# Wider query groups, wider spatial passes, one gelu batch and new durations for the static scheduler of a two-layer attention and gMLP kernel

## Chip, cores, metric

One NeuronCore of one Trainium2 chip (trn2). The metric is the device time of one execution in microseconds (us). Profiles come from one execution of each kernel.

## The reference, cut to what matters

Two layers, each a multi-query attention with 32 heads of 16 and one shared key and value head, then a gated MLP whose gate is a product over all 2048 tokens (the "spatial" product).

```python
def _A_ref(x, wq, wk, wv, wo):                    # S = 2048, D = 512, H = 32, Dh = 16
    q = (x @ wq).reshape(B, S, H, Dh).transpose(0, 2, 1, 3)
    k = x @ wk; v = x @ wv                        # one key/value head for all
    scores = einsum("bhqd,bkd->bhqk", q, k) * Dh ** -0.5
    o = einsum("bhqk,bkd->bhqd", softmax(scores), v)
    return o.transpose(0, 2, 1, 3).reshape(B, S, H * Dh) @ wo

def _B_ref(x, w_in, w_sp, b_sp, w_out):           # Fh = 896
    z = gelu(x @ w_in)
    z1, z2 = z[..., :Fh], layernorm(z[..., Fh:])
    g = einsum("ts,bsf->btf", w_sp, z2) + b_sp[None, :, None]
    return (z1 * g) @ w_out

for _ in range(2):
    x = x + _A_ref(layernorm(x), ...)
    x = x + _B_ref(layernorm(x), ...)
```

## The kernel before

Tokens are handled in chunks of 512, 512, 512, 256, 128 and 128. Per layer, 2048 blocks of scores (128 keys x 512 columns) need an exponential. ScalarE (ACT) takes most of them, three and two banks of PSUM at a time; VectorE (DVE) takes the rest with a chain of seven instructions. Behind this run, on the same engines, the projections, layer norms, gelus and spatial passes of the chunks already done. After the last attention chunk of a layer there is a **closing**, in which the last chunk's MLP, the rest of the spatial products and the output projection must end before the next layer can start.

All this is ordered by a **static list scheduler that runs at build time**. Every operation has a duration; the scheduler simulates the engines with those durations, always takes the ready operation of the best priority, and the resulting order per engine is the program. PE executes strictly in that order. So a charge in this model changes none of the instructions that do the work; it changes where they stand, and with that how many warming matmuls are put in and whether ACT or DVE takes a block. One stream inserts these warming matmuls (results thrown away) wherever the model thinks that PE's activity in the last 3.41 us (a constant of the kernel's code) falls short.

The charges (cut):

```python
def job(self, pieces, cons, ...):             # side work on PE: projections, spatial passes
    ...
    prev = self.op("pe", ..., dur, ...)       # counts dur * 2400 columns of activity

def d_mm(n):                                  # charge for one matmul of n columns
    return max(n, 64) / 2400.0

# fill = the score matmuls of one ACT instruction; n = columns of the chunk, ns = 512 // n
o = k.sc.op("pe", fn, 0.32 + 0.05 * (ns - 1), deps, ..., slow=0.53 + 0.05 * (ns - 1))
# PV of one unit (four heads x 512 columns)
o = k.sc.op("pe", fn, (0.23 if self.u % 2 == 0 else 0.32) + 0.05 * (ns - 1), ...)
```

What a block is in a small chunk, and the wide spatial pass (cut):

```python
def _qk(self, e, b, bank):        # one block: ns key tiles of n columns side by side
    for s, kt in enumerate(b.unit.kts):
        ins = e.matmul(self.b32(bank)[:, s * n:(s + 1) * n],
                       self.kT[32*j:32*j+32, kt*128:(kt+1)*128],
                       self.qs[32*j:32*j+32, g.q.slot, g.qoff:g.qoff + n], tile_position=(32*j, 0), ...)

# spatial: 8 token groups of 256; two feature tiles per PSUM bank; weights double-buffered, 512 KB a load
for tc in range(8):
    ld = self.dma(... self.wsT[:, 8*sl:8*sl+nst, :] <- self.ws_dv[:, s0:s1, tc*256:(tc+1)*256])
    for f0 in range(0, NF, 2):
        ... e.matmul(o_[256 columns], self.z2n[:, s, f*128:(f+1)*128], w) for s in range(s0, s1)

# mixer_chunk: every chunk's gelu on its own, between two table loads
def gl(e):
    e.activation(z1v, z1v, ACTF.Gelu_apprx_tanh)
    return e.activation(z2f[...], z2f[...], ACTF.Gelu_apprx_tanh)
```

The softmax here doesn't subtract the row's maximum and nothing guards it: scores larger than these inputs give would overflow.

Of the kernel before, what the change touches and what calls it, by code (L numbers as in the profile page):

```python
# [57 lines left out]
class Sched:  # L58
# [217 lines left out]
    def job(self, pieces, cons, deps, prio, sem="side", piece_deps=None):  # L276
# [3 lines left out]
        for i, (fn, dur) in enumerate(pieces):  # L280
            dd = list(deps) if i == 0 else [prev]
            if piece_deps is not None:
                dd += piece_deps[i]
            prev = self.op("pe", (lambda e, fn=fn: fn(e, j.bank.idx)), dur, dd, prio if i == 0 else min(prio, CONT), sem=sem, job=j,
                           first=(i == 0), soft=[d for c in cons for d in c.get("deps", ())] if i == 0 else ())
# [79 lines left out]
GPL = 0  # L365
MERGE = 9
# [20 lines left out]
def d_mm(n):  # L387
    return max(n, 64) / 2400.0


class Group:
    __slots__ = ("layer", "ci", "hg", "t0", "n", "units", "q", "qoff", "evac", "index")


class QSet:

    __slots__ = ("groups", "op", "slot", "left", "reads", "index")


class Unit:  # L400
    __slots__ = ("grp", "kts", "blocks", "pv", "index", "last", "first")
# [6 lines left out]
class Kern:  # L408
    def __init__(self, nc, A_x, A_wq, A_wk, A_wv, A_wo, B_x, B_w_in, B_w_sp, B_b_sp, B_w_out, out):
# [12 lines left out]
        self.merge = MERGE  # L422
# [11 lines left out]
        self.ident16 = sb([P, P], FP16, "ident16")  # L434
# [10 lines left out]
        self.b8 = sb([8, 256], BF16, "b8")  # L445
# [26 lines left out]
        self.gp = sb([P, 8, NF, 256], FP16, "gp")  # L472
# [10 lines left out]
        self.ws_n = 0  # L483
# [49 lines left out]
    def load(self, A_x, A_wq, A_wk, A_wv, A_wo, B_b_sp):  # L533
# [20 lines left out]
        self.l_b = self.dma(lambda e: e.dma_start(self.b8[:], B_b_sp.rearrange("(k t) -> k t", k=8)), (), "ldb", 4096)  # L554
# [11 lines left out]
        for tc in range(8):  # L566
            for f in range(NF):
                self.gp_read[(tc, f)] = [o for o in free]
# [7 lines left out]
        self.c_id16 = sc.op("pool", lambda e: e.tensor_copy(self.ident16[:], self.ident[:]), 0.3, [self.c_id], 0.9)  # L576
# [111 lines left out]
    def layer_groups(self, layer):  # L688
        t0 = 0
        for ci, n in enumerate(self.chunks):  # L690
            nsub = 512 // n
            for hg in range(8):
                g = Group()
                g.layer, g.ci, g.hg, g.t0, g.n = layer, ci, hg, t0, n
                g.index = len(self.groups)
                if hg % nsub == 0:
                    qs = QSet()
                    qs.groups, qs.op, qs.left, qs.reads = [], None, 0, []
                    qs.index = len(self.qsets)
                    qs.slot = qs.index % NQS  # L700
                    self.qsets.append(qs)
                g.q = self.qsets[-1]
                g.qoff = (hg % nsub) * n
                g.q.groups.append(g)
                g.units = []
                g.evac = None
                for k in range(self.NT // nsub):
                    u = Unit()
                    u.grp = g
                    u.kts = list(range(k * nsub, (k + 1) * nsub))  # L710
                    u.index = len(self.units)
                    u.first = (k == 0)
                    u.last = (k == self.NT // nsub - 1)
                    u.pv = None
# [7 lines left out]
                g.q.left += 4 * len(g.units)  # L722
# [8 lines left out]
    def q_released(self, q):  # L731
        nx = q.index + NQS
        if nx < len(self.qsets):
            q2 = self.qsets[nx]
            if q2.groups[0].layer == 0 or q2.groups[0].layer == q.groups[0].layer or self.l1_ready:
                self.make_q(q2, q.reads)
            else:
                self.q_wait.append((q2, q.reads))
# [4 lines left out]
    def make_q(self, q, war=()):  # L743
        sc = self.sc
        g = q.groups[0]
        n = g.n

        def pe(e, b, h):
            ins = None
            for g2 in q.groups:  # L750
                for kd in ((0, 1), (2, 3))[h] if n == 512 else range(4):
                    if n == 512 or (g2.hg - g.hg) // (len(q.groups) // 2) == h:
                        ins = e.matmul(self.b32(b)[:, g2.qoff:g2.qoff + n], self.wq_pad[:, kd, g2.hg, :],  # L753
# [7 lines left out]
        pe_last, (op,) = sc.job([((lambda e, b: pe(e, b, 0)), 2 * d_mm(512)), ((lambda e, b: pe(e, b, 1)), 2 * d_mm(512))],  # L761
# [8 lines left out]
    def finish_group(self, g, pv_last):  # L770
        sc = self.sc
        n = g.n
        nq = n // 128
        par = self.evac_n % 2
        self.evac_n += 1
        ev = sc.op("dve", lambda e: e.tensor_copy(self.oT[:, par, 0:n], self.b32(self.pvb)[:, 0:n]), d_psum(n),  # L776
# [3 lines left out]
        def pe(e, b):  # L780
            ins = None
            for qt in range(nq):
                ins = e.transpose(self.b16(b)[:, qt * 128:(qt + 1) * 128], self.oT[:, par, qt * 128:(qt + 1) * 128],
                                  self.ident[:])
            return ins

        def rc(e, b):
            return e.reciprocal(self.rden[:, par, 0:nq, :], self.b16(b)[:, 0:nq * 128].rearrange(
                "p (qt j r) -> p qt j r", qt=nq, j=4)[:, :, :, DH])

        def nm(e, b):
            return e.tensor_tensor(  # L792
                self.on[:, 0:nq, g.hg * 64:(g.hg + 1) * 64].rearrange("p qt (j d) -> p qt j d", d=DH),
                self.b16(b)[:, 0:nq * 128].rearrange("p (qt j r) -> p qt j r", qt=nq, j=4)[:, :, :, 0:DH],
                self.rden[:, par, 0:nq, :, None].to_broadcast([P, nq, 4, DH]), ALU.mult)
        pl, (r, m) = sc.job([(pe, nq * 0.06)], [
            dict(fn=rc, dur=0.09 + nq * 4 * 8.4e-3, prio=0.6, deps=[self.rd_read[par]]),
            dict(fn=nm, dur=d_psum(nq * 64), prio=0.5, deps=[d for qt in range(nq) for d in self.on_read[qt]])],
            [ev, self.c_id], 1.2)
        self.oT_read[par] = pl  # L800
        self.rd_read[par] = m
        g_norm = m
        self.norms.append(g_norm)
        if g.hg == 7:
# [56 lines left out]
    def mixer_chunk(self, g):  # L861
# [37 lines left out]
        c0 = g.t0 % 512 if g.ci == self.merge + 1 else 0  # L899
        z1v = (self.z1L if last else self.z1s[:].rearrange("p (f t) -> p f t", f=NF))[:, :, c0:c0 + n]  # L900
        z1_war = list(self.dx_s.end) if last else list(self.z1s_free)
# [26 lines left out]
        if g.ci == self.merge:  # L928
            self.held = (T, z1, z2)
            return  # L930
        t0 = T[0]
        if g.ci == self.merge + 1:
            T, z1, z2 = [a + b for a, b in zip(self.held, (T, z1, z2))]
            t0, T = T[0], T
            z1v = self.z1s[:].rearrange("p (f t) -> p f t", f=NF)[:, :, 0:128 * len(T)]
# [3 lines left out]
        def gl(e):  # L939
            e.activation(z1v, z1v, ACTF.Gelu_apprx_tanh)  # L940
# [4 lines left out]
        else:  # L945
            gs = z1 = [sc.op("act", gl, d_act(NF * nt * 128) + d_act(nt * FH), z1 + z2, -1.0, table="gelu")] * (2 * nt)
        sp = self.dma(lambda e: e.dma_start(self.z1_dv[:, :, t0 * 128:(t0 + nt) * 128], z1v), z1,
                      f"z1s{g.layer}{g.ci}", nt * P * P * NF * 2)
        if last:
            self.z1L_spill = sp  # L950
        else:
            self.z1s_free = [sp]
        self.z1_spill.append((t0 * 128, (t0 + nt) * 128, sp))
# [15 lines left out]
        for (s0, s1, ci) in self.passes:  # L969
            if ci == g.ci:  # L970
                self.spatial(s0, s1, g.layer, final=False)
        if last:
            self.spatial(self.s_fin, self.NT, g.layer, final=True)
# [8 lines left out]
    def spatial(self, s0, s1, layer, final):  # L982
        sc = self.sc
        acc = s0 > 0
        pr = 2.0 if final else (2.5 if s1 > 8 else 4.0)
        if final:
            self.kv_war_from_layer()
            self.l_wout = self.dma(lambda e: e.dma_start(self.w_out_r, self.w_out_d.rearrange("(c p) n -> p c n", p=P)),
                                   [o for o in self.dx_s.end], "ldw", 917504, pr)
            self.hT_read = [[o for o in self.dx_s.end], [o for o in self.dx_s.end]]  # L990
        z1r = self.z1s[:].rearrange("p (k f t) -> p k f t", k=2, f=NF)
        zl = [list(self.z1s_free), list(self.z1s_free)]
        nst = s1 - s0
        early = not final and nst < 4
        gp_pe = final and layer < GPL
        z2f = self.z2n[:].rearrange("p t f -> p (t f)")
        if early:

            slot0 = self.wsT[:, 0:8, :].rearrange("p s t -> p (s t)")
            self.wsP = []  # L1000
            nf = self.NT - s1
            parts = [(0, 4, z2f[:, 2048:5120], (2, 3, 4, 5)), (4, 6, z2f[:, 5120:6656], (5, 6, 7)),
                     (6, 8, slot0[:, 0:1536], None)]
            if nst == 2:
                parts = [(0, 4, z2f[:, 4096:6144], (4, 5, 6)), (4, 8, slot0, None)]
            for (c0, c1, w_, tiles) in parts:
                w_ = w_.rearrange("p (s t) -> p s t", s=nst)
                war = self.last_ws[0] if tiles is None else [o for t in tiles for o in self.z2_read[t]]
                ld = self.dma(lambda e, w_=w_, c0=c0, c1=c1: e.dma_start(w_, self.ws_dv[:, s0:s1, 256 * c0:256 * c1]),
                              war + self.ws_st[s0:s1], f"wsp{c0}", (c1 - c0) * nst * 65536, 1.0)  # L1010
                for tc in range(c0, c1):
                    self.wsP.append((w_[:, :, 256 * (tc - c0):256 * (tc - c0 + 1)], ld, tiles))
            self.held_f = range(0, 3 if nf == 1 else 5)
            self.wsF = z2f[:, 0:2048 * nf].rearrange("p (s t) -> p s t", s=nf)
            self.wsF_ld = self.dma(lambda e: e.dma_start(self.wsF, self.ws_dv[:, s1:self.NT, :]),
                                   [o for t in self.held_f for o in self.z2_read[t]] + self.ws_st[s1:], "wsf", nf * 524288, 1.5)
        for tc in range(8):
            if final:
                lds = [self.wsF_ld]
                ws = [(s, self.wsF[:, s - s0, tc * 256:(tc + 1) * 256]) for s in range(s0, s1)]  # L1020
                held = self.held_f
            elif early:
# [622 lines left out]
```

## Time and profile before

| | before |
|---|---|
| time | 1915.69 us median of 3 runs (1913.76 to 1916.67) |
| instructions | 41204, of them 17275 matmuls |
| busy share | PE 85%, DVE 93%, ACT 92% |
| mean granted PE clock, profiled run | 0.974 |

From the page of the kernel before: busy time by engine, then groups of instructions. Columns of a group: line, engine, operation, what it writes and reads, count, busy time, mean ns of one, idle time of the engine just before it and who ended most of it.

```profile
PE 1634.2 (85%) x17275; PEld 655.4 (34%) x17275; DVE 1774.8 (93%) x3265; ACT 1767.6 (92%) x1573; POOL 59.3 (3%) x106
...
L1305 ACT ACTIVATE Pa<-ps_all 128x1536 bf16<-128x1536 f32 (+1 forms) x1437 | 1643.0, 1348 | 56.9 <-PE ps_all L1591 46.4
L1591 PE MATMUL ps_all<-qs,kT 32*128 32x512 bf16 (+2 forms) x6144 | 577.7, 317 | 225.6 <-ACT Pa L1305 207.8
...
L1488 DVE TENSOR_SCALAR E<-ps_all 128x512 int32<-128x512 f32 x505 | 343.7, 684 | 28.2 <-PE ps_all L1591 25.9
```

ACT's exponentials (line 1305) and DVE's (505 blocks, begun by line 1488) fill both engines. ACT does 4096 - 505 = 3591 blocks in 1643 us: 0.457 us each.

Where the time is lost is seen by stage. The windows view of the kernel before; each row is a stretch, its length, the busy time of each engine in it, the granted PE clock and the DMA load. The stretches: chunk 0's end and chunk 1; the wide spatial pass; the small chunks; then, in layer 1, chunk 0 undisturbed, chunk 1 with gelus, the wide pass, the small chunks; last the closing.

```profile
core 0: us, PE busy (x) PEld busy (x) DVE busy (x) ACT busy (x) POOL busy (x), PEclk, DMA share, GB/s
300.00:555.00 255.00, 205.67 (x1543) 58.38 (x1544) 246.62 (x431) 243.76 (x206) 6.70 (x8) 0.95 0.04 12
555.00:785.00 230.00, 216.41 (x2343) 97.04 (x2343) 208.83 (x368) 219.12 (x186) 3.55 (x6) 0.97 0.08 23
785.00:906.00 121.00, 104.49 (x2393) 65.41 (x2392) 102.89 (x215) 116.88 (x103) 4.46 (x8) 0.97 0.17 52
1022.00:1247.00 225.00, 182.47 (x1456) 49.64 (x1456) 222.60 (x381) 224.20 (x200) 2.27 (x4) 1.00 0.00 1
1247.00:1503.00 256.00, 212.12 (x1598) 60.64 (x1596) 237.19 (x410) 247.55 (x211) 6.13 (x8) 0.95 0.04 13
1503.00:1667.00 164.00, 156.23 (x1621) 70.38 (x1619) 149.00 (x259) 156.69 (x136) 1.88 (x4) 1.00 0.08 23
1667.00:1853.00 186.00, 158.76 (x3110) 91.34 (x3109) 161.79 (x326) 178.72 (x154) 6.63 (x10) 0.95 0.13 41
1853.00:1915.00 62.00, 53.40 (x405) 33.98 (x402) 53.10 (x126) 19.39 (x39) 1.56 (x4) 1.00 0.28 83
```

The undisturbed stretch 1022 to 1247 has ACT busy 99.6% at full clock: nothing to gain there. In the six other attention stretches ACT is idle 11.2 + 10.9 + 4.1 + 8.5 + 7.3 + 7.3 = 49.3 us (length less busy time).

The waits of the kernel before (engine, line, whom it waited for: us in total, times, longest):

```profile
ACT Pa L1305 <- PE ps_all L1591: 46.4, 93, 2.4
ACT E L1107 <- PE ps_all L1066: 43.2, 10, 8.1
...
DVE st_19 L956 <- ACT z2n L941: 10.4, 8, 2.6
```

The first is exponentials waiting for score matmuls, the second is the closing.

What narrow matmuls cost is read from start to start in PE's timeline (start, us to the modelled end, what, count), here in a 128-column chunk of the kernel before:

```profile
851.34 0.42 PE L1591 MATMUL ps_all<-qs,kT 32*128 32x128 bf16 x12
851.70 0.41 PE L1384 MATMUL ps_all<-Pa,V 128*32 128x128 bf16 x16
852.04 0.61 PE L1066 MATMUL ps_all<-wsT,z2n 128*128 128x256 bf16 x4
```

Twelve score matmuls of 128 columns (three blocks) hold PE for 0.36 us; the median over all such fills is 0.353 us, against 0.323 us for three matmuls of 512. The scheduler charged this fill 0.47.

One gelu in ACT's timeline of the kernel before: two table loads around two gelus, 8.9 us without an exponential.

```profile
1261.27 1.28 ACT L940 ACT_TABLE_LOAD   x1
1262.56 3.19 ACT L940 ACTIVATE z1s<-z1s 128x3584 bf16<-128x3584 bf16 x1
1265.66 3.17 ACT L941 ACTIVATE z2n<-z2n 128x3584 bf16<-128x3584 bf16 x1
1268.85 1.28 ACT L1305 ACT_TABLE_LOAD   x1
```

### The profile page before, as it was taken

What the parts mean: (1) busy time and instruction counts of PE and PEld (TensorE: products, weight loads), DVE (VectorE), ACT (ScalarE), POOL (GpSimd) and SP (SyncE); (2) the same over time, 40 slices, a digit from 0 to 9 for tenths busy, and PEclk for the clock granted to TensorE, in tenths of its full rate; (3) what the DMA queues carried; (4) which work ended last, traced back from release to release, by engine and by line L of the source; (5) the groups of instructions that cost most, each with busy time, mean ns of one, the idle gap of its engine ahead of it and who ended that gap; (6) DMA issues with size and microseconds to landing.
All of it is one profiled execution on the core that took longest, in us unless ns stands there. A gap on an engine that the chain in (4) does not pass through costs nothing.

```text
span 1914.8 us, 41204 instructions
## 1 busy us (share of the span) xinstructions
PE 1634.2 (85%) x17275; PEld 655.4 (34%) x17275; DVE 1774.8 (93%) x3265; ACT 1767.6 (92%) x1573; POOL 59.3 (3%) x106
## 2 busy tenths in 40 slices
PE   6887887788889998988988788888788999988898
PEld 3222222122234443555642122222122444335564
DVE  7999999999998898987999999989999898989968
ACT  6999999999999999999389999999999999999973
POOL 3000000000000000000010000000000000000000
PEclk9999999999999999999999999989998999999899
DMA  9700001000010100022200000010000010000213
GB/s 265 192 1 1 1 1 42 1 1 1 1 31 23 34 7 26 14 64 59 64 1 1 1 1 1 1 42 1 1 1 20 23 34 18 8 26 14 64 54 107
DMA packets 98041, 59.83 MB, mean 31 GB/s; under 512 B 39736, under 2 KB 94272, under 8 KB 97856
## 3 DMA queue, kind: packets, MB, share of 16 engines
q1 hardware_dynamic: 96272, 56.64, 10.5%
q8 instruction: 137, 2.24, 0.5%
q10 hardware_dynamic: 1584, 0.56, 0.1%
q14 instruction: 48, 0.39, 0.1%
HBM read 30.97 MB, written 17.83 MB: 25 GB/s over the span
## 4 chain that ended last, share of the span: by engine, by line
ACT 34%; PE 28%; DVE 24%; issue 12%; POOL 1%; ACTq 0%; DVEq 0%; POOLq 0%
ACT Pa L1305 32%; PE ps_all L1591 8%; PE ps_all L1066 7%; PE ps_all L1384 5%; DVE E L1488 4%; DVE Pd L1526 3%; DVE E L1524 2%; DVE E L1521 2%; DVE E L1515 2%; PE ps_all L1574 2%; PE ps_all L1135 2%; ACT z2n L941 1%; PE ps_all L753 1%; DVE E L1518 1%; DVE gp L1090 1%
## 5 line engine op out<-in xcount | busy, mean ns | idle before, releaser
L1305 ACT ACTIVATE Pa<-ps_all 128x1536 bf16<-128x1536 f32 (+1 forms) x1437 | 1643.0, 1348 | 56.9 <-PE ps_all L1591 46.4
L1591 PE MATMUL ps_all<-qs,kT 32*128 32x512 bf16 (+2 forms) x6144 | 577.7, 317 | 225.6 <-ACT Pa L1305 207.8
L1591 PEld LDWEIGHTS ps_all<-qs,kT 32*128 32x128 bf16 x6144 | 173.7, 93 | 710.4 <-ACT Pa L1305 627.7
L1488 DVE TENSOR_SCALAR E<-ps_all 128x512 int32<-128x512 f32 x505 | 343.7, 684 | 28.2 <-PE ps_all L1591 25.9
L1384 PE MATMUL ps_all<-Pa,V 128*32 128x512 bf16 (+2 forms) x5421 | 332.7, 317 | 2.1 <-DVE oT L776 1.6
L1526 DVE SCALAR_TENSOR_TENSOR Pd<-E 128x1024 uint16<-128x1024 int32 (+1 forms) x253 | 306.8, 1213 | 0.8
L1574 PE MATMUL ps_all<-wo_r,zero 128*128 128x512 bf16 (+2 forms) x923 | 250.0, 371 | 2.2 <-DVE E L1488 1.8
L1066 PE MATMUL ps_all<-wsT,z2n 128*128 128x256 bf16 x1428 | 216.4, 278 | 6.0 <-DVE on L792 2.7
L1384 PE MATMUL ps_all<-Pd,V 128*32 128x512 bf16 (+2 forms) x723 | 182.5, 327 | 0.0
L1521 DVE TENSOR_TENSOR E<-E 128x1024 f16<-128x1024 f16 (+1 forms) x253 | 172.9, 683 | 3.3
L1524 DVE TENSOR_TENSOR E<-E 128x1024 f16<-128x1024 f16 (+1 forms) x253 | 172.6, 682 | 2.3
L1515 DVE TENSOR_SCALAR E<-E 128x1024 f16<-128x1024 uint16 (+1 forms) x253 | 172.7, 684 | 1.1
L1066 PEld LDWEIGHTS ps_all<-wsT,z2n 128*128 128x128 bf16 x1428 | 117.2, 98 | 74.3 <-issue 35.6
L1384 PEld LDWEIGHTS ps_all<-Pa,V 128*32 128x32 bf16 x5421 | 98.8, 96 | 119.4 <-issue 101.6
L1574 PEld LDWEIGHTS ps_all<-wo_r,zero 128*128 128x128 bf16 x923 | 70.2, 99 | 121.3 <-issue 91.3
L1518 DVE TENSOR_SCALAR E<-E 128x1024 f16<-128x1024 f16 (+1 forms) x253 | 105.6, 417 | 2.6
L1517 DVE TENSOR_SCALAR E<-E 128x1024 f16<-128x1024 f16 (+1 forms) x253 | 105.6, 417 | 2.2
L1090 DVE TENSOR_TENSOR gp<-ps_all,gp 128x512 f16<-128x512 f32 (+1 forms) x128 | 76.2, 615 | 18.1 <-PE ps_all L1066 17.7
L753 PE MATMUL ps_all<-xnTA,wq_pad 128*128 128x512 bf16 (+2 forms) x384 | 69.9, 311 | 2.2 <-DVE E L1488 2.0
L1107 ACT ACTIVATE E<-ps_all 128x512 f16<-128x512 f32 (+1 forms) x58 | 26.2, 563 | 43.2 <-PE ps_all L1066 43.2
L881 PE MATMUL ps_all<-w_in_r,xnTB 128*128 128x448 bf16 x256 | 63.2, 356 | 2.0 <-DVE E L1488 1.2
L910 PE MATMUL ps_all<-xnTB,w_in_r 128*128 128x512 bf16 (+2 forms) x336 | 62.9, 311 | 1.3 <-DVE z1s L921 1.0
(83 smaller groups left out, 1171.1 us busy)
## 6 DMA issues: line engine op xcount, KB each, us to landing
wsT_scratch<-gp SPq DMA_DIRECT2D x16, 512.0 KB, 3.7
wsT<-wsT_scratch SPq DMA_DIRECT2D x16, 512.0 KB, 4.0
z1s<-z_scratch SPq DMA_DIRECT2D x16, 448.0 KB, 3.9
z_scratch<-z1s SPq DMA_DIRECT2D x6, 896.0 KB, 4.0
wsT<-wsT_scratch SPq DMA_DIRECT2D x16, 256.0 KB, 2.9
X<-in_A_x_dram SPq DMA_DIRECT2D x8, 256.0 KB, 6.6
out_dram<-X SPq DMA_DIRECT2D x16, 128.0 KB, 1.7
w_in_r<-in_B_w_in_dram SPq DMA_DIRECT2D x1, 1792.0 KB, 10.9
```

What stands on the lines that cost most here:

```text
L1066: ins = e.matmul(o_, self.z2n[:, w[0], f * 128:(f + 1) * 128], w[1], start=st, stop=sp_)
L1305: return e.activation(k.Pa[:, base:base + n, :], k.b32(b0, n).rearrange("p (k q) -> p k q", k=n), ACTF.Exp, scale=SCALE)
L1384: ins = e.matmul(k.b32(k.pvb)[32 * j:32 * j + 32, 0:n], k.V[:, kt, 32 * j:32 * j + 32], b.slot[:, s * n:(s + 1) * n], tile_position=(0, 32 ...
L1488: return k.sc.op("dve", lambda e: e.tensor_scalar(k.eI[:, s, 512 * i:512 * (i + 1)], k.b32(j.bank.idx)[:, 0:512], C_LOG2, C_BIAS, op0=ALU. ...
L1515: return lambda e: e.tensor_scalar(out, a, m, None, op0=ALU.mult)
L1517: return lambda e: e.tensor_scalar(out, a, b, None, op0=ALU.add)
L1518: return lambda e: e.tensor_scalar(out, a, m, b, op0=ALU.mult, op1=ALU.add)
L1521: o4 = sc.op("dve", lambda e: e.tensor_tensor(q, u, w, ALU.mult), d_sb(n, 0.521e-3), [o3], pr)
L1524: o6 = sc.op("dve", lambda e: e.tensor_tensor(q, q, u, ALU.mult), d_sb(n, 0.521e-3), [o5], pr)
L1526: o7 = sc.op("dve", lambda e: e.scalar_tensor_tensor(po.bitcast(U16), I, 2.0 ** -9, q, op0=ALU.mult, op1=ALU.add), d_sb(n, 1.042e-3), [o6] ...
L1574: ins = e.matmul(k.b32(k.pvb if b is None else b.idx)[:, 0:n], k.zero[:], k.wo_r[:, 0, 0:n], start=b is not None, stop=b is not None)
L1591: ins = e.matmul(self.b32(bank)[:, s * n:(s + 1) * n], self.kT[32 * j:32 * j + 32, kt * 128:(kt + 1) * 128], self.qs[32 * j:32 * j + 32, g ...
```

## The change

Four parts:

- **Groups**: in a small chunk, 2 or 4 head groups lie side by side as 512 query columns against one key tile, so that every score and PV matmul is 512 wide. With it the extra charge for narrow fills and PV units goes.
- **Spatial**: the spatial passes take 512 tokens per matmul (4 token groups in place of 8, one feature tile per bank, the widest pass with a single-buffered 1 MB weight load).
- **Merge**: chunk 0's gelu waits for chunk 1's; both run between one pair of table loads.
- **Durations**: the scheduler's charges for side matmuls, and the columns that it counts for them.

```diff
             prev = self.op("pe", ...,
-                           first=(i == 0), ...)
+                           cols=dur * 1900.0, first=(i == 0), ...)      # Durations
 def d_mm(n):
-    return max(n, 64) / 2400.0
+    return max(n / 2400.0 + 0.006, min(0.045 + n * 0.43e-3, 0.155))
 ... layer_groups:                                                        # Groups
-            nsub = 512 // n
-            for hg in range(8):
+            nh = 512 // n
+            for hg in range(0, 8, nh):
-                for k in range(self.NT // nsub):
-                    u.kts = list(range(k * nsub, (k + 1) * nsub))
+                for k in range(self.NT):
+                    u.grp, u.kt, u.index, u.pv = g, k, len(self.units), None
 ... fill and PV:
-        o = k.sc.op("pe", fn, 0.32 + 0.05 * (ns - 1), deps, ...)
+        o = k.sc.op("pe", fn, 0.32, deps, ...)
-        o = k.sc.op("pe", fn, (0.23 if self.u % 2 == 0 else 0.32) + 0.05 * (ns - 1), ...)
+        o = k.sc.op("pe", fn, 0.23 if self.u % 2 == 0 else 0.32, ...)
 ... mixer_chunk:                                                         # Merge
-        if g.ci == self.merge:          # merge was 9: never
+        if g.ci == 0:
+            self.held = (T, z1, z2, z1v)                                 # z1 kept in gp's place
+            return
+        if g.ci == 1:
+            T, z1, z2 = [a + b for a, b in zip(self.held[:3], (T, z1, z2))]
 ... spatial:                                                             # Spatial
-        for tc in range(8):
-            for f0 in range(0, NF, 2):  # 256 columns
+        nsl = 1 if nst > 4 else 2
+        for tc in range(4):
+            for f in range(NF):         # 512 columns
(cut: storage of gp and bias, the closing split off as its own method, the group's finish)
```

## The prediction

> **What bounds the kernel.** The page gives ScalarE (ACT) 92% and VectorE (DVE) 93% busy over 1914.8 us, PE 85%. Both evaluate the softmax exponentials: by the groups, 1437 ACT ops (1643 us, 2.5 blocks of 512 columns each, 0.457 us a block) and 505 DVE blocks (seven ops, about 2.7 us a block). In the undisturbed stretch 1000-1260 (the windows) ACT is busy 99.6%, DVE 98%: 2.55 blocks/us. It falls to 2.3 in the two wide spatial passes (560-720, 1480-1640; PE 154 of 160 us) and 2.1-2.3 in the small chunks (720-900, 1640-1840; DVE idle about 40 us in all, ACT 14). Over both attention phases ACT idles about 58 us; 46 us of it "exp waits for the score matmuls" (the waits). The two closings (ACT idle about 75 us) are hardly touched.
>
> **What the change does.**
> 1. QK and PV fall from 6144 to 4096 matmuls each. Start-to-start times in the trace say that this saves little PE time: three score blocks take 0.323 us at 512 wide, 0.331 as six of 256, 0.352 as twelve of 128; two PV units 0.548, 0.554, 0.563. Over about 300 such fills: some 6 us of PE, with PV under 2, off the critical path. The Trainium skill ("TensorE: Matmul & The Clock Gate", Back-to-back issue gap) gives N/2.4 + 2.5 ns warm; the trace agrees (0.109 us per 256-wide spatial matmul): columns, not instructions, are paid.
> 2. Spatial passes: half the matmuls, twice as wide. Four of 256 with the switch take 0.543 us; two of 512 (the w_in groups) 0.538. No gain. The 8-tile weight load becomes single-buffered 1 MB (512 KB lands in 4 us): three gaps of perhaps 8 us per layer, which only spread the pass.
> 3. Finishing small head groups: 48 become 16 in both layers, about 7 us of DVE less, worth 1-2 us, since DVE does a seventh of the exponentials. Fewer waits of PV for the evacuation.
> 4. Gelu of chunks 0 and 1 together: one pair of 1.283 us table loads less per layer: 5.1 us of ACT, on the path, worth 4.5. Against it: one ACT stall of about 15 us in place of two of 9; DVE, whose blocks come only with fills, idles 2.4 us in one of 9 and will idle some 8.
> 5. The static schedule is built with other PE durations. It charged small-chunk fills 0.37/0.47 us against 0.33/0.35 in the trace; afterwards 0.32, about right. Better ordering may recover part of the ACT idle time in small chunks and spatial passes (32 us) and at gelus: I take 8 us. Side matmuls count as fewer columns, so a few more warming matmuls.
>
> **Sum.** 4.5 (tables) + 1.5 (DVE) + 8 (ordering, fewer group ends) + 2 (PE relief feeding DVE) - 1.5 (longer gelu stall) = 14.5 us, 0.8%.
>
> Predicted 1901 us, range 1882 to 1917. Faster by over 2%: 0.10; within 2%: 0.87; slower by over 2%: 0.03.
>
> **What would show it.** Table loads at the gelu line 10 -> 8; QK and PV 4096 each; PE busy down only a few per cent, still near 96% in the spatial stretches; DVE evacuations 96 -> 64; ACT exp still 0.457 us a block; steady stretch still 2.55 blocks/us; small-chunk stretches shorter by 5-10 us in both layers together; closings the same to 3 us.
>
> **What would make it wrong.** If narrow matmuls hold PE longer than starts show, the gain reaches 30-40 us. If the merged gelu lets the clock fall, or the single-buffered passes drag spatial work into the closing, it vanishes. The schedule is a greedy list: any change of durations reshuffles it, a few us either way.

## The result, and the profile after

| | before | after |
|---|---|---|
| time, median | 1916.18 us (4 runs, 1913.76 to 1919.03) | 1885.68 us (4 runs, 1884.69 to 1889.73) |
| ratio | 1 | 0.9844 (95%: 0.9824 to 0.9865) |
| matmuls | 17275 | 12178 |
| mean granted clock, fast runs | 0.9755 (40 runs) | 0.982 (4 runs) |

The change makes the kernel 1.6% faster, 30 us.

The page of the kernel after, same rows as before:

```profile
PE 1613.0 (85%) x12178; PEld 497.1 (26%) x12178; DVE 1750.5 (93%) x3129; ACT 1763.4 (93%) x1570; POOL 58.2 (3%) x101
...
L1288 ACT ACTIVATE Pa<-ps_all 128x1536 bf16<-128x1536 f32 (+1 forms) x1440 | 1642.9, 1345 | 33.4 <-PE ps_all L1559 28.7
L1559 PE MATMUL ps_all<-qs,kT 32*128 32x512 bf16 x4096 | 567.9, 390 | 206.4 <-ACT Pa L1288 193.4
...
L1464 DVE TENSOR_SCALAR E<-ps_all 128x512 int32<-128x512 f32 x499 | 339.7, 684 | 24.0 <-PE ps_all L1559 22.5
```

A third of the score matmuls is gone, yet their busy time falls only from 577.7 to 567.9 us. The exponentials are as many and as long (1642.9 us for 3597 blocks). What fell is the idle time before them.

The windows view of the kernel after, stretches cut at the same numbers of blocks:

```profile
core 0: us, PE busy (x) PEld busy (x) DVE busy (x) ACT busy (x) POOL busy (x), PEclk, DMA share, GB/s
295.00:543.00 248.00, 205.54 (x1545) 56.83 (x1544) 237.84 (x417) 244.05 (x207) 4.84 (x6) 0.97 0.03 8
543.00:768.00 225.00, 209.12 (x1571) 65.06 (x1568) 210.67 (x363) 217.51 (x186) 3.68 (x6) 0.98 0.08 26
768.00:886.00 118.00, 106.62 (x795) 33.73 (x792) 107.60 (x190) 115.58 (x101) 4.76 (x8) 0.97 0.15 45
1008.00:1235.00 227.00, 183.14 (x1466) 49.81 (x1464) 223.19 (x380) 224.31 (x199) 3.23 (x4) 0.99 0.00 1
1235.00:1479.00 244.00, 202.73 (x1548) 56.48 (x1549) 231.78 (x403) 242.62 (x207) 1.87 (x4) 0.97 0.03 9
1479.00:1640.00 161.00, 151.71 (x1152) 46.04 (x1152) 152.54 (x268) 156.36 (x137) 4.76 (x6) 0.98 0.05 14
1640.00:1825.00 185.00, 169.38 (x1217) 52.20 (x1215) 164.41 (x290) 179.31 (x152) 7.43 (x10) 0.96 0.15 48
1825.00:1888.00 63.00, 48.07 (x261) 22.31 (x259) 44.90 (x107) 19.20 (x39) 1.56 (x4) 0.95 0.28 81
```

Row by row against before: 7, 5 and 3 us in layer 0; -2, 12, 3 and 1 us in layer 1; the closing of layer 1 is the same (62 and 63). The time before the first row (300 and 295 us) gains 5, some 2 of it because 5 fewer blocks are done. The closing of layer 0 with the start of layer 1 (906 to 1022 before, 886 to 1008 after) gives back 6. The stretch that gained most is chunk 1 with the gelus, in both layers, where no score or PV matmul has changed its width and spatial work has barely begun (11 us of PE before, 3 after): 19 us of the 27 between the two profiled runs. In the six disturbed stretches ACT is now idle 3.9 + 7.5 + 2.4 + 1.4 + 4.6 + 5.7 = 25.5 us, 24 us less.

The waits after:

```profile
ACT E L1103 <- PE ps_all L1091: 31.9, 6, 8.9
ACT Pa L1288 <- PE ps_all L1559: 28.7, 64, 1.4
...
DVE st L962 <- ACT z2n L943: 15.9, 5, 7.4
```

Exponentials wait 18 us less for score matmuls. The third line is the price of the merge: DVE stands still for up to 7.4 us during the long gelu, where it was 2.6.

The merged gelu in ACT's timeline after: one stall of 14.9 us, one pair of loads.

```profile
1453.82 1.28 ACT L942 ACT_TABLE_LOAD   x1
1455.11 3.19 ACT L942 ACTIVATE gp<-gp 128x3584 bf16<-128x3584 bf16 x1
1458.21 3.17 ACT L942 ACTIVATE z1s<-z1s 128x3584 bf16<-128x3584 bf16 x1
1461.29 6.16 ACT L943 ACTIVATE z2n<-z2n 128x7168 bf16<-128x7168 bf16 x1
1467.47 1.28 ACT L1288 ACT_TABLE_LOAD   x1
```

And a fill in a small chunk after, three blocks of 512 in 0.32 us (start to start):

```profile
850.32 0.39 PE L1559 MATMUL ps_all<-qs,kT 32*128 32x512 bf16 x3 [0.41 <-ACT Pa L1288]
850.64 0.62 PE L911 MATMUL ps_all<-xnTB,w_in_r 128*128 128x128 bf16 x8
```

### The profile page after: what moved, and what is told of

It is laid out like the page before. It is cut to its first block, busy times and chain, and to the rows that moved or that the text cites. A ratio compares the mean times of both kernels' runs of the same rounds, so it can differ in the third digit from the quotient of the medians.

```text
span 1887.9 us, 30817 instructions
## 1 busy us (share of the span) xinstructions
PE 1613.0 (85%) x12178; PEld 497.1 (26%) x12178; DVE 1750.5 (93%) x3129; ACT 1763.4 (93%) x1570; POOL 58.2 (3%) x101
## 4 chain that ended last, share of the span: by engine, by line
ACT 35%; PE 26%; DVE 25%; issue 13%; POOL 1%; ACTq 0%; POOLq 0%
ACT Pa L1288 32%; PE ps_all L1036 7%; PE ps_all L1559 7%; PE ps_all L1363 4%; DVE E L1464 4%; DVE Pd L1502 3%; PE ps_all L1123 2%; DVE E L1500 2%; DVE E L1491 2%; DVE E L1497 2%; PE ps_all L1545 1%; DVE st L596 1%; ACT z2n L943 1%; DVE z2n L886 1%; DVE E L1494 1%
## 5 line engine op out<-in xcount | busy, mean ns | idle before, releaser
L1288 ACT ACTIVATE Pa<-ps_all 128x1536 bf16<-128x1536 f32 (+1 forms) x1440 | 1642.9, 1345 | 33.4 <-PE ps_all L1559 28.7
L1559 PE MATMUL ps_all<-qs,kT 32*128 32x512 bf16 x4096 | 567.9, 390 | 206.4 <-ACT Pa L1288 193.4
L1363 PE MATMUL ps_all<-Pa,V 128*32 128x512 bf16 x3597 | 324.3, 391 | 0.1
L1502 DVE SCALAR_TENSOR_TENSOR Pd<-E 128x1024 uint16<-128x1024 int32 x250 | 303.4, 1214 | 0.9
L1545 PE MATMUL ps_all<-wo_r,zero 128*128 128x512 bf16 x818 | 256.2, 391 | 0.6 <-DVE E L1464 0.2
L1036 PE MATMUL ps_all<-wsT,z2n 128*128 128x512 bf16 x714 | 198.9, 388 | 3.5 <-DVE gp L1048 2.4
L1363 PE MATMUL ps_all<-Pd,V 128*32 128x512 bf16 x499 | 176.6, 390 | 0.0
L1497 DVE TENSOR_TENSOR E<-E 128x1024 f16<-128x1024 f16 x250 | 170.9, 684 | 3.3
L1500 DVE TENSOR_TENSOR E<-E 128x1024 f16<-128x1024 f16 x250 | 170.4, 682 | 1.9
L1491 DVE TENSOR_SCALAR E<-E 128x1024 f16<-128x1024 uint16 x250 | 170.9, 684 | 1.3
L1493 DVE TENSOR_SCALAR E<-E 128x1024 f16<-128x1024 f16 x250 | 104.6, 418 | 2.2
L1494 DVE TENSOR_SCALAR E<-E 128x1024 f16<-128x1024 f16 x250 | 104.3, 417 | 2.1
L1048 DVE TENSOR_TENSOR gp<-ps_all,gp 128x512 f16<-128x512 f32 x112 | 75.5, 685 | 20.3 <-PE ps_all L1036 20.0
```

Of the source, the lines that this page charges most:

```text
L1036: ins = e.matmul(self.b32(b), self.z2n[:, s, f * 128:(f + 1) * 128], w_[:, s - s0, :], start=st, stop=sp)
L1288: return e.activation(k.Pa[:, base:base + n, :], k.b32(b0, n).rearrange("p (k q) -> p k q", k=n), ACTF.Exp, scale=SCALE)
L1363: ins = e.matmul(k.b32(k.pvb)[32 * j:32 * j + 32, :], k.V[:, u.kt, 32 * j:32 * j + 32], b.slot, tile_position=(0, 32 * j), start=u.first, ...
L1491: return lambda e: e.tensor_scalar(out, a, m, None, op0=ALU.mult)
L1493: return lambda e: e.tensor_scalar(out, a, b, None, op0=ALU.add)
L1494: return lambda e: e.tensor_scalar(out, a, m, b, op0=ALU.mult, op1=ALU.add)
```

## The experiments

Twelve kernels ran, all with 5 rounds, all correct. They are made from the four parts (the new PE durations are called the model in the labels), and by my own check, with all parts off or all on the generated program is that of the kernel before or after, instruction for instruction. Merge alone on the kernel before could not be built, since its scheduler found no free bank. The runs come from three chips, each with the kernel before beside it (medians 1915.4 to 1915.9 us), so ratios compare them best. "Columns left" below counts, in the trace, the columns of spatial matmuls of the earlier passes that start after a layer's last score matmul, without the 14,336 that belong to the closing anyway; the expectations quote figures that include these (for no_groups 69,000 and 94,000; the 64,000 that one expectation gives for its layer 0 is not what the trace shows). "Tail" is the time from layer 1's last score matmul to the end.

| kernel | ratio to before (95%) | median us | columns left, layer 0 / 1 | tail us |
|---|---|---|---|---|
| before | 1 | 1916 | 44,000 / 41,000 | 63 |
| after | 0.9844 (0.9824-0.9865) | 1886 | 17,000 / 17,000 | 64 |
| no_spatial512 | 0.9856 (0.9836-0.9877) | 1888 | 26,000 / 36,000 | 63 |
| no_gelu_merge | 0.9853 (0.9834-0.9873) | 1890 | 18,000 / 20,000 | 65 |
| no_model | 0.9889 (0.9870-0.9908) | 1897 | 13,000 / 17,000 | 65 |
| no_groups | 1.0025 (1.0006-1.0044) | 1921 | 54,000 / 80,000 | 84 |
| no_groups_honest | 0.9871 (0.9855-0.9888) | 1890 | 37,000 / 20,000 | 62 |
| after_false_charge | 0.9906 (0.9887-0.9925) | 1897 | 43,000 / 47,000 | 66 |
| before_honest | 1.0014 (0.9999-1.0030) | 1918 | 36,000 / 29,000 | 63 |
| before_groups | 1.0073 (1.0055-1.0091) | 1928 | 16,000 / 15,000 | 64 |
| before_model | 1.0176 (1.0159-1.0194) | 1949 | 71,000 / 61,000 | 78 |
| groups_model | 0.9925 (0.9910-0.9940) | 1902 | 30,000 / 29,000 | 64 |
| groups_model_nudged | 0.9928 (0.9914-0.9941) | 1901 | 34,000 / 37,000 | 64 |
| after_more_warm | 0.9872 (0.9853-0.9890) | 1892 | 22,000 / 20,000 | 64 |

### One part taken out of the new kernel

My first theory was the prediction's: width buys nothing, table loads and ordering buy all. The rivals were that the wide spatial pass, or the narrow matmuls themselves, hold PE.

**no_spatial512** (spatial part back to 256 columns):
```diff
-        for tc in range(4):
-            for f in range(NF):             # 512 columns
+        for tc in range(8):
+            for f0 in range(0, NF, 2):      # 2 x 256 columns, double-buffered loads
```

> The new kernel with the spatial passes put back to 256 columns (double-buffered weight loads, two feature tiles per job), all else new. Theory 1 (the columns are what PE pays; width gains nothing, as the prediction said): within 3 us of the new kernel, about 1886 us. Theory 2 (read from the exponential-progress comparison: each layer's wide pass gained 6 us although PE time per column is equal): about 12 us slower than the new kernel, 1898 us, with ACT below 95% busy again in the wide-pass stretch.

Measured 1888.36 us: 2 us from the new kernel, inside the intervals. Theory 1 held. My reading from the progress of blocks (the times at which every 64 blocks were done, in both kernels) fell: the gain in the wide pass isn't due to the width.

**no_gelu_merge**:
```diff
-        if g.ci == 0:
+        if g.ci == -1:                      # chunk 0's gelu runs alone again
             self.held = (T, z1, z2, z1v)
```

> The new kernel with the gelu of chunk 0 run alone as before, all else new; 12 ACT table loads at gelu and exp lines come back to 10 and 10. Prediction's account: 3 us slower (4.5 of table loads less 1.5 of a longer stall). From the progress comparison, 3 to 4 us per layer: 7 us slower, about 1893 us.

Measured 1889.56 us: 2 to 4 us, again not clear of the intervals. It is in line with the prediction's 3 us but does not confirm it.

**no_model** (Durations back, everything else new):
```diff
-                           cols=dur * 1900.0, first=(i == 0), ...
+                           first=(i == 0), ...
-    return max(n / 2400.0 + 0.006, min(0.045 + n * 0.43e-3, 0.155))
+    return max(n, 64) / 2400.0
```

> The new kernel with the old PE durations and column counts in its own static scheduler (instructions the same, their order not). If the better durations bring what the prediction took for ordering: up to 8 us slower, 1894 us. If the gain lies in the instructions: within 3 us of the new kernel.

Measured 1896.68 us: 11 us slower by the medians, 9 by the ratios, with the same work in another order (830 warming matmuls against 818, and 3 more blocks on ACT, follow from the order).

**no_groups** (small chunks as before, with their old charges):
```diff
-            for hg in range(0, 8, nh):      # 512 query columns, one key tile
+            for hg in range(8):             # n query columns, 512 // n key tiles
-        o = k.sc.op("pe", fn, 0.32, ...)
+        o = k.sc.op("pe", fn, 0.32 + 0.05 * (ns - 1), ...)
```

> The new kernel with the small chunks' head groups kept apart as before (6144 score and 6144 PV matmuls), all else new. If narrow matmuls cost only what their start-to-start times show (0.01 to 0.03 us a fill, 7 us of DVE): 3 to 5 us slower than the new kernel, about 1890 us. If narrow matmuls hold a saturated PE: 12 us slower or more.

Measured 1921.43 us: 36 us slower, slower even than the kernel before. That looks like a saturated PE. But until the end of layer 0's attention its blocks are done within 5 us of the new kernel's, narrow chunks included (I compared the times at which every 64 blocks were done); nearly all is lost in the two closings. The source view of the spatial matmuls in the tail, first this kernel:

```profile
1836.00:1920.00 84.00, 35.95 (x157) 14.55 (x156) 0.98 0.24 73
```
then the new kernel:
```profile
1824.00:1888.00 64.00, 7.96 (x33) 2.99 (x33) 0.95 0.27 80
```

157 spatial matmuls of the earlier passes (36 us) were still to be done when the attention ended, against 33 (8 us). ACT's longest wait in the closing shows it, from the waits of this kernel:

```profile
ACT E L1103 <- PE ps_all L1091: 59.3, 8, 21.6
```

Two causes fit: narrow matmuls took PE's time, or the scheduler only believed so and put the spatial work late.

### True and false charges

**no_groups_honest** changes no working instruction of no_groups, only the charges, to what the trace of the kernel before shows. (A second charge for the same matmuls, `slow`, which the model takes where it expects a throttled clock, keeps its old 0.05.)
```diff
-        o = k.sc.op("pe", fn, 0.32 + 0.05 * (ns - 1), ...)
+        o = k.sc.op("pe", fn, 0.32 + 0.01 * (ns - 1), ...)
-        ... (0.23 if self.u % 2 == 0 else 0.32) + 0.05 * (ns - 1), ...
+        ... (0.23 if self.u % 2 == 0 else 0.32) + 0.003 * (ns - 1), ...
```

> The run without grouped heads took 1921 us; here the same narrow instructions, but the static scheduler charges them what the trace shows (a fill 0.33 or 0.35 us in place of 0.37 or 0.47, a PV unit 0.003 to 0.009 us over the wide one in place of 0.05 to 0.15). Theory A (the hardware pays almost nothing for narrow matmuls; the loss was the false charge, which left spatial work to the closing): about 1890 us, and the spatial columns left after a layer's last fill fall from 64,000 and 94,000 to about 30,000. Theory B (narrow matmuls really hold PE): 1912 us or more, and the columns left stay.

Measured 1889.85 us: 32 us faster than no_groups by the medians, 30 by the ratios; 4 to 5 us from the new kernel, which is not clear of the intervals. Spatial work in its tail, same view:

```profile
1829.00:1891.00 62.00, 9.54 (x40) 3.59 (x40) 0.97 0.27 83
```

This decides between the two: 4096 more narrow matmuls, with the group ends that go with them, cost 4 to 5 us, if anything; the false charge cost about 30. Part of these 30 is warming: no_groups has 1059 warming matmuls with 458,000 columns, this kernel 937 with 437,000. The 21,000 columns between them are some 9 us of PE (an estimate, at 512 columns per 0.216 us).

**after_false_charge** is the mirror: wide instructions, the old false charges.
```diff
-        o = k.sc.op("pe", fn, 0.32, deps, ...)
+        o = k.sc.op("pe", fn, 0.32 + 0.05 * (blocks[0].unit.grp.nh - 1), deps, ...)
-        ... 0.23 if self.u % 2 == 0 else 0.32, ...
+        ... (0.23 if self.u % 2 == 0 else 0.32) + 0.05 * (u.grp.nh - 1), ...
```

> The new kernel with its wide instructions, but the scheduler charges small-chunk fills 0.37 and 0.47 us and PV units 0.05 and 0.15 us extra, as the kernel before did. Theory A: about as slow as the run without grouping, 1915 us, with 60,000 or more spatial columns left at each closing. Theory B (the wide instructions themselves bring the gain): within 6 us of the new kernel, 1886 us.

Measured 1896.82 us: 11 to 12 us slower. The direction is theory A's, the size is a third of what I expected: the columns left rose to 47,000 but stayed below the point from which the closing grows (see below).

**before_honest** makes the same correction in the kernel before:
```diff
+        o = k.sc.op("pe", fn, 0.32 + 0.01 * (ns - 1), ...)       # and 0.003 for PV
```

> The kernel before, instructions the same, only the charges for narrow fills and PV units made true. Theory A: 10 to 20 us faster than before, about 1900 us. Theory B: within 4 us of before.

Measured 1918.08 us, ratio 1.0014: nothing. Here theory A failed. With the old durations for side work, true fill charges alone do not help (`slow` again kept its 0.05).

**before_groups** (Groups alone on the kernel before):

> The kernel before with grouped heads alone (old spatial passes, gelus and PE durations). Theory A: as the kernel before with true charges, about 1900 us, at most 5 us better for the fewer group ends. Theory B: about 1890 us, well below the kernel before with true charges.

Measured 1928.41 us: 12 to 14 us slower, against both theories. Its mean granted clock was 0.971, lower than 0.976 of the kernel before, and exponentials waited 50.3 us for score matmuls (46.4 before). The edit is the Groups part of the diff above.

The table now shows a threshold. With up to 47,000 columns left, the tail is 62 to 66 us; with 61,000 and 80,000 it is 78 and 84. The closing seems to have room for some 50,000 columns while it waits for its own chain (an estimate: the bound lies between 47,000 and 61,000; 50,000 columns at the 512 per 0.216 us of the runs of 512-wide matmuls are 21 us). The kernel before was just below.

### Two parts together, and the clock

**before_model** (Durations alone) and **groups_model** (Durations and Groups) use those parts of the diff on the kernel before.

> The kernel before with only the new PE durations and column counts in its scheduler; instructions the same, narrow fills still charged 0.37 and 0.47 us. If the durations alone bring most of the gain: 1895 to 1900 us. If they need the true fill charges that come with grouped heads (as the run without groups, 1921 us, suggests): 1910 to 1925 us, with over 60,000 spatial columns left at a closing.

> The kernel before with grouped heads and the new durations together, but old spatial passes and separate gelus. If these two together are the gain (removing the spatial width or the gelu merge from the new kernel cost only 3 us each): 1890 to 1895 us. If spatial width and merge carry it: 1905 us or more.

before_model took 1949.48 us, 33 us slower than before and 24 us beyond the worst that I expected: new side durations with false fill charges leave 71,000 and 61,000 columns to the closings. groups_model took 1901.65 us, 14 us faster than before, but 7 us outside the range that I expected. So Groups alone costs 12, Durations alone costs 33, both gain 14: the parts do not add up. And Spatial and Merge, worth 2 to 4 us each at the end, are worth 13 to 14 us each when added first to groups_model (from 0.9925 to 0.9853 and 0.9856). Either one gains most of it; the second adds little.

The times at which blocks were done show where Durations act. From the 256th to the 1664th block of each layer, that is over chunk 1 and the wide pass, the sums of the windows view over both layers are, for the kernel before, for before_model and for the new kernel:

```profile
sum 1195.00, PE 1024.30 PEld 342.07 DVE 1135.55 ACT 1158.27 POOL 21.13; mean PE 512.15 PEld 171.03 DVE 567.77 ACT 579.13 POOL 10.56
sum 1167.00, PE 999.65 PEld 325.37 DVE 1122.73 ACT 1149.77 POOL 21.44; mean PE 499.83 PEld 162.68 DVE 561.36 ACT 574.89 POOL 10.72
sum 1166.00, PE 996.66 PEld 285.89 DVE 1121.15 ACT 1148.22 POOL 18.87; mean PE 498.33 PEld 142.95 DVE 560.57 ACT 574.11 POOL 9.43
```

So Durations alone, with the working instructions of the kernel before, bring 28 of the 29 us that the whole change brings there, and ACT's idle time falls from 36.7 to 17.2 us (17.8 in the new kernel). The clock does not explain it: before_honest took 1194 us there at a clock of 0.982, groups_model 1177 at 0.975. What has moved is spatial work: 227,000 columns of it start in these stretches in the kernel before, 176,000 in before_model, 184,000 in the new one. The rest must go elsewhere. The small chunks take 123,000 columns in the kernel before and, still with false fill charges, 127,000 in before_model; the remainder falls to the closings, and before_model loses 18 us in the small chunks, 34 in layer 0's closing with the start of layer 1 and 15 in the tail. In the new kernel the small chunks take 217,000 columns in the time they took before (367 and 369 us). This fits with Durations and Groups gaining only together. They are not the only way: no_model, with the old durations, took 1172 us in the same stretches though 213,000 columns start there, so Spatial and Merge bring most of it too, by a way that I have not found; before_groups, which has neither, took 1200.

The new side charges are not simply truer than the old ones. Start to start between fills, two side matmuls of 512 columns take 0.538 us, four of 256 take 0.543 and eight of 128 some 0.55. The old durations charge each of these 0.427; the new ones charge 0.439, 0.620 and 0.800.

**groups_model_nudged** asks whether that 13 us is luck of the order:
```diff
-        o = k.sc.op("pe", fn, 0.32, deps, ...)
+        o = k.sc.op("pe", fn, 0.323, deps, ...)      # the trace's median, 1% more
```

> The kernel before with grouped heads and the new durations (1902 us), and one nudge without meaning of its own: a fill is charged 0.323 us in place of 0.320. It reorders the whole static schedule. If the 13 to 15 us by which adding either the spatial width or the gelu merge improved on that kernel are theirs: it stays within 4 us of 1902 us. If they are largely luck of the greedy order: it moves by 6 us or more, in either direction, and parts of that size cannot be told apart by single runs.

Measured 1901.15 us: no change, although most of PE's order had changed. One nudge isn't a distribution, but it speaks for the 13 us being theirs. Why either suffices stays open.

**after_more_warm** tests the clock. Over 64 runs of the 13 kernels other than before, runs of the same kernel with a granted clock higher by 0.01 were 10.7 us shorter (pooled slope about each kernel's mean; correlation -0.92). The new kernel's clock is 0.0065 above the old one's: by that slope, and if the clock is the cause, an estimate of 7 of the 30 us. Could one buy more?
```diff
-WARM = 800.0
+WARM = 1400.0
```

> The new kernel with the warming matmuls' margin raised from 800 to 1400 columns (1105 warming matmuls in place of 818). Within each kernel, runs whose granted clock was 0.01 higher were 11 us shorter. If the clock causes that: the mean clock rises from 0.982 to about 0.99 and the time falls to about 1878 us. If time only goes with the clock, or the extra PE work costs as much: 1886 us or slower, with more ACT idle for score matmuls.

Measured 1892.28 us, 5 to 6 us slower, at a mean clock of 0.988; the intervals overlap a little, so it is not faster, and that it is slower is not quite shown. The clock rose as intended; 287 more warming matmuls on PE seem to cost what it gave, or more. The waits for score matmuls did not rise (27.0 us against 28.7), so how they would cost it isn't shown. No experiment pointed to a version that beats the new kernel.

## Why the prediction was right or wrong, point by point

The time, 1886 us, lies in the predicted range, but the range was wide: it ran from no gain at all to one of 34 us. The gain, 30 us, is twice the 14.5 us of the sum, so the range was met partly by luck. By the prediction's own test ("the gain reaches 30-40 us") a gain of this size would even have spoken for costly narrow matmuls; no_groups_honest shows that it was not they.

- **Point 1, narrow matmuls cost almost nothing on PE: right.** no_groups_honest with its 4096 extra matmuls is 4 to 5 us slower than the new kernel, not clear of the intervals. The predicted 8 us of PE time, credited with 2 us, are of that size.
- **Point 2, spatial width: no gain, right** for the finished kernel (2 us, within noise); added to groups_model it was 14 us, which I had not foreseen.
- **Point 3, fewer group ends: not measured alone.** DVE evacuations of PV fell from 96 to 64 as said; the effect is inside the 4 us of point 1.
- **Point 4, merged gelu: in line, though not clear of the noise.** The loads at the gelu line fell from 10 to 8, DVE stood still for 7.4 us in the long gelu (predicted some 8), and the removal cost 2 to 4 us (predicted 3).
- **Point 5, the order: the mis-sized term.** The prediction said: "Better ordering may recover part of the ACT idle time ... I take 8 us". In the disturbed stretches ACT's idle time fell from 49.3 to 25.5 us. ACT does 2.19 of the 2.55 blocks/us, so 24 us of idle time are worth about 0.86 x 24 = 20 us (an estimate, and it holds whatever removed the idle time, not the charges alone). With 4.5 us for table loads and a few for DVE that makes up the gain. That charges can do such things is shown: with equal work they moved the time by some 10 us (no_model), 11 us (after_false_charge) and 30 us (no_groups to no_groups_honest), and in before_model they alone brought 28 of the 29 us of chunk 1 and the wide pass. The prediction named the small chunks, the spatial passes and the gelus; the gain came in the last two, and it went with a move of spatial work into the small chunks, which the prediction did not name.
- **Two sub-points were off.** The gain was not in the small chunks (4 us of the predicted 5 to 10) but in the chunk-1 stretches (19 us), where only the order, the merge, the clock and a little spatial work differ. And I treated the parts as a sum; they interact by more than the whole gain.
- **The signs:** exponential 0.457 us a block and undisturbed rate (571 blocks in 227 us, 2.52; before 574 in 225, 2.55) close to the prediction; the tail within 1 us; PE in the wide-pass stretches 93 to 94% busy, not 96.

Open: how the 20 us divide in the finished kernel between charges, clock, Spatial and Merge, since Durations alone bring them in the early stretches and so, nearly, do Spatial and Merge without Durations; and why Groups alone made the kernel slower.

## What to carry to other kernels

In a statically scheduled kernel, read the charges against start-to-start times in the trace before changing instructions: false charges cost about 30 us here, as much as the whole change gained, while a third fewer score and PV matmuls gained 4 to 5, if anything. But judge a charge by the order that it makes: true fill charges alone gained nothing (before_honest), and the side charges that helped are not nearer to the trace. In a trace of each variant, see where the deferred work goes. Take parts out of the finished version and also put them in alone; here two parts made the old kernel slower when put in alone, and the new one slower when taken out. Work pushed behind the main loop is free only until it outlasts the chain that runs there anyway: here about 50,000 matmul columns, by the layer-1 tails of these kernels.

## What the Trainium skill lacked or had wrong

- "TensorE: Matmul & The Clock Gate", Back-to-back issue gap: it gives two figures for a stream of 512-wide matmuls, 131 ns each "sustained" and N/2.4 + 2.5 = 216 ns "isolated". Here, in the kernel before, 28 of them in a row, each with its own weight load, took 6.05 us from the first start to the start of the next piece: 0.216 us each. Only the second formula fits.
- The same page, Terms, gives the penalty of throttled time as that time x (1 - K/N), half of it at K/N = 4/8. The clock records here do show only 0.5 and 1. By that rule 0.01 less mean clock, which is 38 us more at half clock (0.02 of 1900 us), would cost 19 us; over the 64 runs it went with 10.7 us, about 0.28 of the 38. PE is only one of three busy engines in this kernel, which may be why; that is not shown.
- "TensorEngine Tiling (Array Packing)", Key Properties, says that a change of tiling mode drains the TensorE, with no figure. Here a piece of two 512-wide full-array matmuls between row-tiled fills takes 0.538 us where 2 x 0.216 = 0.432 were due: about 0.1 us a switch (an estimate). The scheduler's charges for 512-wide pieces, 0.427 old and 0.439 new, both lack it.
- "ScalarE: Activation LUTs", What ACT_TABLE_LOAD costs: 1283 ns agrees to the nanosecond; the drain of about 1380 ns that it adds to every switch does not show. In the kernel before, the load at 1261.27 began 0.02 us after an exponential ended, it ended at 1262.55, and the gelu began at 1262.56.
